# Turning the sink probabilities with VectorE and GpSimd blocks in place of TensorE transposes

## The chip, the cores and the metric

One core of one Trainium2 chip runs the whole program. The metric is the device time of one execution in microseconds (us). The kernel before takes 730.89 us (median of 3 runs, 730.44 to 731.45).

## What is computed

Attention with a few sink positions and a sliding window, then a feed-forward block over the result. q, k and v are 4 batches x 8 heads x 768 positions x 64; `n_sink` is 4 and `window` is 128. Cut to what matters:

```python
scores = (1 / np.sqrt(D)) * q @ k.transpose(0, 1, 3, 2)
keep = (pos[None, :] < n_sink) | ((rel >= 0) & (rel < window))
a = softmax(np.where(keep, scores, -1e9))
x = (a @ v).transpose(0, 2, 1, 3).reshape(B * S, H * D)      # 3072 x 512
h = x @ w_in                                                 # 512 -> 2048
out = (h * sigmoid(h)) @ w_out                               # 2048 -> 512
```

## The kernel before

The 3072 tokens are cut into 8 chunks of 384 (batch, half of the sequence). A chunk goes through two stages: attention for its four pairs of heads (32 periods p = 0 to 31, four to a chunk), then the feed-forward block over its 16 slices of d_ff (`mlp1`, `act`, `mlp2`). The attention of one chunk is computed while the feed-forward block of the chunk before it runs, so that the two share the engines.

The first two chunks (periods 0 to 7, `f_...` functions) do attention in a simpler way; the change does not touch it. From period 8 on (24 periods) each operand is split in two parts, a rounded one (type F32R, "hi") and the rest ("lo"), and products are made of both. For one period, with two heads j = 0 and 1:

- `q_prep`, `k_prep` (lines 387 to 428): VectorE turns 32x32 blocks of q and k into PSUM, ScalarE writes the hi part, VectorE the lo part, and two copies (lines 402, 403) by GpSimd or, from period 15 on, by VectorE.
- `v_prep` (430): the split of v, and of the v rows of the sink slots (`vsn`, NS = 8 slots for each head) into `vk`; vsn holds its rows twice, for the hi and the lo part of P.
- `scores` (451): 2 products for each 128-row tile, reduced by VectorE into `pm`, whose row of 264 holds 128 columns of the window's block before, 8 sink slots and 128 own columns.
- `softmax` (493): ScalarE's exp, VectorE adds the first 128 columns to the own ones (line 502), GpSimd multiplies the own columns by 1/sum (505), and line 508 writes the sink slots of P, scaled, into a small tile `sx`, 8 slots for each head and tile.
- `ptrans` (513): three TensorE transposes of the own columns, ScalarE (528) and VectorE (530) split them, and GpSimd's affine selects (535, 539) part them in two triangles, four for each head.
- `strans` (544): the sink slots of both heads, 16 columns a tile, are transposed by TensorE (line 550, one for each of 3 tiles, or 2 in the first half of a sequence, t0 = 1) into a PSUM bank `sk`; ScalarE (557) writes the hi part to partitions 0 to 15 of `pst`, VectorE (558) the lo part to partitions 32 to 47.
- `av` (562): products of v with the triangles (577, 586) and one more, line 593, of `vk` with `pst`, all into one PSUM bank, which lines 601 to 605 evict. Each head waits for `pst`.

Of the 24 periods, 16 lie in a second half (3 tiles) and 8 in a first half (2 tiles).

The order of the work is set by a planner at the end of the function (lines 930 to 997): each stage is given a due time in units, where one unit is one slice of the feed-forward block (`mlp1` and `mlp2`); all stages are sorted by their time and emitted in that order. The times of attention stand in `OPT["a"]`, relative to T of the period, four units to a period: `st` for strans, `av0` and `av1` for the two heads of av, `q`, `k`, `v`, `s`, `sm` for the preparations, scores and softmax. A scheduler below takes that order as priority, so that an instruction that is ready may pass one that is not; on each engine the instructions then run in the order that it left. GpSimd, VectorE, ScalarE and TensorE each have one queue, and all loads and stores here go through SP's.

Of the kernel before, what the change touches and what calls it, by code (L numbers as in the profile page):

```python
# [8 lines left out]
F32 = mybir.dt.float32  # L9
F32R = mybir.dt.float32r  # L10
I32 = mybir.dt.int32
AF = mybir.ActivationFunctionType
ALU = mybir.AluOpType
# [7 lines left out]
NS = 8  # L21
# [5 lines left out]
OPT = dict(  # L27
    S=7.901, s0=0.903, f_l=2.468, f_p=-1.643, f_v=3.079, f_sm=0.693, f_pt=0.795, f_av=0.251,
    tk=15.973, s1=1.65, F1=1.024, D0=2.076, w=[0.458, 8.623, 11.237, 18.573], wd=[0.85, 0.58,
    1.293, 0.67], wc=19.252, wcd=2.681, warm=7, wg=4, ord=1, edge=8, dua=15, adp=0, glp=0,  # L30
    ptv=7, fill=[0, 4, 0, 0, 1, 0, 0, 2], na=[2, 16], lod=[6, 32], nv=[0, 0], hid=[0, 0],
    ktd=[0, 0], a=dict(load=-3.44, q=-0.196,
    k=-0.079, v=1.975, s=1.356, sd=0.613, sm=1.795, smd=0.457, pt0=2.725, st=3.866, pt1=3.355,
    av0=4.289, av1=4.426), m0=dict(act=0.108, m2=1.206), m=dict(act=1.023, m2=1.546), fin=0.772,
)


# [132 lines left out]
def attn_moe_kernel(  # L170
# [11 lines left out]
    nc = tc.nc  # L182
    B, H, S, D = q.shape
# [5 lines left out]
    P = 128  # L189
    HP = H // 2  # L190
    CT = 384
    NTB = CT // P
# [10 lines left out]
    ident = const.tile([P, P], F32, name="ident")  # L203
# [26 lines left out]
    with ExitStack() as fast:  # L230
        wpool = fast.enter_context(tc.tile_pool(name="wpool", bufs=1))
        p1 = fast.enter_context(tc.tile_pool(name="p1", bufs=1))
# [3 lines left out]
        ps_a = fast.enter_context(tc.tile_pool(name="ps_a", bufs=3, space=PSUM))  # L236


        m0 = p1.tile([P, P], F32, name="m0")
        m1 = p1.tile([P, WIN], F32, name="m1")  # L240
        m2 = p1.tile([P, WIN], F32, name="m2")
        rel = p2.tile([P, P], F32, tag="xh0", name="rel")
        col = p2.tile([P, P], F32, tag="xh1", name="col")
        sk = p2.tile([P, P], F32, tag="xh2", name="sk")
# [39 lines left out]
        ksA = p1.tile([P, HP, B, NS], F32R, name="ksA")  # L284
        ksB = p1.tile([P, HP, B, NS], F32R, name="ksB")

        vsn = p1.tile([48, H, D], F32, tag="vsn2", name="vsn")


        zero = {}  # L290
# [40 lines left out]
        st = [dict() for _ in range(NPER)]  # L331


        turns = [(b, half) for b in range(B) for half in range(NHALF)]
# [3 lines left out]
        def geo(p):  # L338
            c, hp = divmod(p, HP)
            b, half = turns[c]  # L340
            return c, b, half, hp
# [36 lines left out]

        def load_vs(b):
            for j in range(2):  # L380
                for r in (0, 32):
                    nc.sync.dma_start(
                        vsn[r + 8 * j : r + 8 * j + 8, j::2, :],
                        v[b, j::2, 0:NS, :].rearrange("h j d -> j h d"),
                    )
# [19 lines left out]
        def k_prep(p):  # L405
# [11 lines left out]
            for j, src in ((0, ksA), (1, ksB)):  # L417
# [4 lines left out]
                )  # L422
            A = ksv[:, 0, j0:, :P]
            Bk = ksv[:, 1, j0:, :P]
# [5 lines left out]
        def v_prep(p):  # L430
            c, b, half, hp = geo(p)
            s = st[p]
            j0 = 0 if half else 1
            vs = p1.tile([P, NTB + 1, 2, 2, D], F32R, tag="vs", name=f"vs{p}")
            s["vs"] = vs
            vn = s["vn"]
            for j in range(2):
                nc.scalar.copy(vs[:, j0:, j, 0, :], vn[:, j0:, j, :])  # L438
            for j in range(2):
                nc.gpsimd.tensor_tensor(  # L440
                    vs[:, j0:, j, 1, :], vn[:, j0:, j, :], vs[:, j0:, j, 0, :], ALU.subtract
                )
            if "vk" not in zero:
                zero["vk"] = p1.tile([P, 2, 2, D], F32R, tag="vk", name="vk")
                nc.gpsimd.memset(zero["vk"].bitcast(F32), 0.0)
            vk = zero["vk"]
            src = vsn[:, 2 * hp : 2 * hp + 2, :]
            nc.scalar.copy(vk[:48, :, 0, :], src)
            nc.gpsimd.tensor_tensor(vk[:48, :, 1, :], src, vk[:48, :, 0, :], ALU.subtract)

        def scores(p, j):
            c, b, half, hp = geo(p)
# [40 lines left out]
        def softmax(p, j):  # L493
            c, b, half, hp = geo(p)
            s = st[p]
            pm = s["pma", j]
            t0 = 0 if half else 1
            r = exps(p, j)

            own = pm[:, t0:, SEG:]  # L500
            eng = nc.gpsimd if p < OPT["adp"] else nc.vector
            eng.tensor_tensor(own, own, pm[:, t0:, :P], ALU.add)
            for t in range(NTB):
                x = pm[:, t, SEG:]
                nc.gpsimd.tensor_scalar(x, x, r[:, t : t + 1], 1.0, ALU.mult, ALU.mult)  # L505
            if j == 0:
                s["sx"] = p1.tile([P, NTB, 2, NS], F32, tag="sx", name=f"sx{p}")
            nc.gpsimd.tensor_tensor(
                s["sx"][:, t0:, j], pm[:, t0:, P : P + NS],
                r[:, t0:].unsqueeze(2).to_broadcast([P, NTB - t0, NS]), ALU.mult,  # L510
            )

# [29 lines left out]
                )  # L542

        def strans(p):
            c, b, half, hp = geo(p)
            s = st[p]
            t0 = 0 if half else 1
            pt = ps_a.tile([P, 512], F32, tag="at", name=f"sk{p}")
            for t in range(t0, NTB):
                nc.tensor.transpose(  # L550
                    pt[0 : 2 * NS, t * P : (t + 1) * P],
                    s["sx"][:, t].rearrange("p h j -> p (h j)"),
                    ident,
                )
            ps = zero["pst"]
            src = pt[0 : 2 * NS, t0 * P : CT]
            nc.scalar.copy(ps[0 : 2 * NS, t0 * P :], src)
            nc.vector.tensor_tensor(
                ps[32 : 32 + 2 * NS, t0 * P :], src, ps[0 : 2 * NS, t0 * P :], ALU.subtract
            )  # L560

        def av(p, j):
            c, b, half, hp = geo(p)
            s = st[p]
            if j == 0:
                s["x32"] = p1.tile([P, 4 * P], F32, tag="x32", name=f"x32_{p}")
            o = ps_a.tile([P, 512], F32, tag="at", name=f"o{p}_{j}")
            pq = s["pq", j].rearrange("p t o x q -> p (t o) x q")

            todo = [(1, 1, 3, 0), (2, 3, 5, P)] + [(0, 0, 1, 0)] * half  # L570
            merge = p >= OPT["edge"]
            if not merge:
                todo.append((3, 5, 6, 2 * P))
            first = True
            for kb, b0, b1, q0 in todo:
                for x in range(2):
                    nc.tensor.matmul(  # L577
                        o[:, q0 : q0 + (b1 - b0) * P].rearrange("p (b q) -> p b q", q=P),
                        s["vs"][:, kb, j].rearrange("p a d -> p (a d)"),
                        pq[:, b0:b1, x],  # L580
                        start=first, stop=False, skip_group_check=True,
                    )
                    first = False
            if merge:

                nc.tensor.matmul(  # L586
                    o[:, 2 * P : 4 * P],
                    s["vs"][:, NTB, j].rearrange("p a d -> p (a d)"),
                    pq[:, 5].rearrange("p x q -> p (x q)"),
                    start=False, stop=False, skip_group_check=True,  # L590
                )
            t0 = 0 if half else 1
            nc.tensor.matmul(  # L593
                o[:, t0 * P : CT],
                zero["vk"][:, j].rearrange("p a d -> p (a d)"),
                zero["pst"][:, t0 * P :],
                start=False, stop=True, skip_group_check=True,
            )
            x32 = s["x32"][64 * j : 64 * j + 64]
            n = 4 * P if merge else CT  # L600
            nc.scalar.copy(x32[:, :n], o[64:128, :n])
            nc.vector.tensor_tensor(x32[:, :n], o[0:64, :n], x32[:, :n], ALU.add)
            if merge:
                nc.vector.tensor_tensor(
                    x32[:, 2 * P : CT], x32[:, 2 * P : CT], x32[:, CT:], ALU.add
                )
            if j == 1:
                s["xh"] = p2.tile([P, CT], F32R, tag=f"xh{hp}", name=f"xh{p}")
                s["xl"] = p2.tile([P, CT], F32R, tag=f"xl{hp}", name=f"xl{p}")
                x32 = s["x32"][:, :CT]  # L610
                nc.scalar.copy(s["xh"], x32)
                nc.vector.tensor_tensor(s["xl"], x32, s["xh"], ALU.subtract)
# [16 lines left out]
        for n in range(2):  # L629
            zero["pT", n] = p2.tile([P, 2, 2 * NTB, P], F32, tag="pq", name=f"pTz{n}")  # L630
            nc.gpsimd.memset(zero["pT", n][:, :, 2], 0.0)
        FP = 2 * HP

        def f_load(p):
            c, b, half, hp = geo(p)
# [295 lines left out]
        for p in range(NPER):  # L931
            T = O["S"] + 4.0 * (p - HP)
            c, b, half, hp = geo(p)
            if p < FP:
                for j in range(2):
# [20 lines left out]
                       lambda p=p, j=j: in_turn(lambda: f_av(p, j)))  # L956
                continue
            A = O["a"]

            tl = T - 4.0 + max(A["k"] + 0.05, 4.0 + A["load"])  # L960
            tv = T - 4.0 + max(A["v"] + 0.05, 4.0 + A["load"])
            at(tl, lambda p=p: load(p))
            at(tv, lambda p=p: load_v(p))
            if hp == 0 and (c == 2 or b != turns[c - 1][0]):
                at(max(tv, O["tk"]) + 0.02, lambda b=b: load_vs(b))
            at(T + A["q"], lambda p=p: q_prep(p))
            at(T + A["k"], lambda p=p: k_prep(p))
# [66 lines left out]
```

## Time and profile before

| | us |
|---|---|
| median of 3 runs | 730.89 |
| lowest, highest | 730.44, 731.45 |
| the profiled execution | 731.18 |
| its span, first to last instruction | 729.4 |

The span covers 12276 instructions; the mean granted TensorE clock over it is 0.995 of full speed. In the rows, PE is TensorE's matmul, PEld its weight load, DVE is VectorE, ACT ScalarE, POOL GpSimd. Line numbers (L550) are those of the kernel before. `x16` behind a row is a count of instructions. The chain of waits follows the work that ended last back from the last instruction, at each step to what released it; its pieces carry the time that each adds to the chain. A busy TensorE is not TensorE at its peak, because the ends of matmuls are modelled; the chain's pieces and the starts are the better guide.

### The profile page before, as it was taken

What the parts mean: (1) busy time and instruction counts of PE and PEld (TensorE: products, weight loads), DVE (VectorE), ACT (ScalarE), POOL (GpSimd) and SP (SyncE); (2) the same over time, 40 slices, a digit from 0 to 9 for tenths busy, and PEclk for the clock granted to TensorE, in tenths of its full rate; (3) what the DMA queues carried; (4) which work ended last, traced back from release to release, by engine and by line L of the source; (5) the groups of instructions that cost most, each with busy time, mean ns of one, the idle gap of its engine ahead of it and who ended that gap; (6) DMA issues with size and microseconds to landing.
All of it is one profiled execution on the core that took longest, in us unless ns stands there. A gap on an engine that the chain in (4) does not pass through costs nothing.

```text
span 729.4 us, 12276 instructions
## 1 busy us (share of the span) xinstructions
PE 714.4 (98%) x3906; PEld 629.8 (86%) x3906; DVE 489.7 (67%) x1323; ACT 498.3 (68%) x1165; POOL 249.1 (34%) x547
## 2 busy tenths in 40 slices
PE   7998999999999999999999999999999999999997
PEld 5676788798999999899999998999898989998986
DVE  5899767977767687667867777677866776731111
ACT  4889788776776777777676767777677777732112
POOL 3310000155444564534334545333443453320000
PEclk8999999999999999999999999999999999999999
DMA  7556446535322542124322352115421321001001
GB/s 177 178 156 183 139 119 164 158 85 147 96 40 41 137 116 61 27 60 133 86 40 40 99 144 62 29 32 164 120 40 26 98 68 32 1 0 44 1 2 45
DMA packets 141333, 61.87 MB, mean 85 GB/s; under 512 B 130000, under 2 KB 130000, under 8 KB 141264
## 3 DMA queue, kind: packets, MB, share of 16 engines
q1 hardware_dynamic: 140976, 61.04, 32.8%
q8 instruction: 32, 0.52, 0.3%
q14 instruction: 37, 0.30, 0.1%
q10 hardware_dynamic: 288, 0.00, 0.0%
HBM read 54.72 MB, written 6.29 MB: 84 GB/s over the span
## 4 chain that ended last, share of the span: by engine, by line
PE 88%; DMA 4%; DVE 4%; ACT 2%; SPq 1%; issue 1%; POOL 0%; DVEq 0%; ACTq 0%
PE h L854 35%; PE out L882 12%; PE out L881 12%; PE out L880 12%; PE o L577 4%; PE s L464 2%; PE s L468 2%; PE o L790 2%; PE pt L519 2%; DMA wraw<-in_moe_w_in_dram 2%; DMA wraw<-in_moe_w_out_dram 2%; PE o L593 1%; PE o L586 1%; PE sk L550 1%; DVE wcv L43 1%; PE s L722 1%
## 5 line engine op out<-in xcount | busy, mean ns | idle before, releaser
L854 PE MATMUL h<-xh,winh 128*128 128x384 f32 x512 | 178.3, 348 | 0.0
L854 PE MATMUL h<-xl,winh 128*128 128x384 f32 x512 | 173.8, 339 | 0.0
L854 PE MATMUL h<-xh,winl 128*128 128x384 f32 x512 | 173.7, 339 | 0.0
L880 PE MATMUL out<-wouth,gh 128*128 128x512 f32 x384 | 153.5, 401 | 1.7 <-ACT gh L865 1.6
L881 PE MATMUL out<-woutl,gh 128*128 128x512 f32 x384 | 152.4, 397 | 0.3 <-DVE woutl L830 0.2
L882 PE MATMUL out<-wouth,gl 128*128 128x512 f32 x384 | 149.9, 396 | 0.1
L865 ACT ACTIVATE gh<-h 128x384 fp32r<-128x384 f32 x128 | 63.1, 493 | 113.7 <-PE h L854 109.8
L868 DVE TENSOR_TENSOR gl<-sg,gh 128x384 fp32r<-128x384 f32 x128 | 73.5, 574 | 88.6 <-ACT sg L866 86.1
L854 PEld LDWEIGHTS h<-xh,winh 128*128 128x128 f32 x512 | 96.5, 188 | 3.5 <-issue 0.9
L854 PEld LDWEIGHTS h<-xl,winh 128*128 128x128 f32 x512 | 96.4, 188 | 2.1
L854 PEld LDWEIGHTS h<-xh,winl 128*128 128x128 f32 x512 | 96.0, 188 | 0.5 <-issue 0.3
L882 PEld LDWEIGHTS out<-wouth,gl 128*128 128x128 f32 x384 | 71.8, 188 | 17.4 <-DVE gl L868 0.8
L880 PEld LDWEIGHTS out<-wouth,gh 128*128 128x128 f32 x384 | 72.2, 188 | 14.6 <-ACT gh L865 2.4
L881 PEld LDWEIGHTS out<-woutl,gh 128*128 128x128 f32 x384 | 72.2, 188 | 12.8 <-DVE woutl L830 1.1
L472 DVE CUSTOM_DVE_ANT_0 pm<-s,m 128x264 f32<-128x264 f32 (+1 forms) x144 | 53.7, 409 | 35.2 <-PE s L468 35.2
L485 ACT ACTIVATE pm<-pm,mx 128x264 f32<-128x264 f32 (+1 forms) x144 | 70.9, 494 | 2.7
L505 POOL TENSOR_SCALAR pm<-pm,r 128x128 f32<-128x128 f32 x144 | 59.0, 427 | 32.6 <-DVE r L490 29.9
L440 POOL TENSOR_TENSOR vs<-vn,vs 128x256 fp32r<-128x256 f32 (+1 forms) x48 | 34.3, 716 | 94.4 <-ACT vs L438 82.5
L866 ACT ACTIVATE sg<-h 128x384 f32<-128x384 f32 x128 | 62.4, 487 | 0.6
L535 POOL TENSOR_SCALAR_AFFINE_SELECT pq<-pq 128x384 fp32r<-128x384 f32 (+1 forms) x96 | 48.2, 502 | 21.0 <-ACT pq L528 20.5
L539 POOL TENSOR_SCALAR_AFFINE_SELECT pq<-pq 128x384 fp32r<-128x384 f32 (+1 forms) x96 | 50.5, 526 | 12.0 <-DVE pq L530 5.6
L530 DVE TENSOR_TENSOR pq<-pt,pq 128x384 fp32r<-128x384 f32 x48 | 26.7, 556 | 30.9 <-ACT pq L528 29.1
(162 smaller groups left out, 1265.8 us busy)
## 6 DMA issues: line engine op xcount, KB each, us to landing
wraw<-in_moe_w_in_dram SPq DMA_DIRECT2D x16, 512.0 KB
wraw<-in_moe_w_out_dram SPq DMA_DIRECT2D x16, 512.0 KB
wchk<-in_moe_w_in_dram SPq DMA_DIRECT2D x16, 512.0 KB
wchk<-in_moe_w_out_dram SPq DMA_DIRECT2D x16, 512.0 KB
qn<-in_q_dram SPq DMA_DIRECT2D x96, 48.0 KB
kn<-in_k_dram SPq DMA_DIRECT2D x64, 64.0 KB
vn<-in_v_dram SPq DMA_DIRECT2D x32, 128.0 KB
out_dram<-ost SPq DMA_DIRECT2D x7, 512.0 KB
```

The source lines that it names most:

```text
L472: nc.vector.tensor_tensor_reduce(out=pm[:, t, off:], in0=sp[:, :w], in1=(m0, m1, m2)[min(blk, 2)], scale=-0.125, scalar=3.0e38, op0=ALU.ad ...
L485: nc.scalar.activation(x, x, AF.Exp, bias=mx[:, p, j * NTB + t : j * NTB + t + 1], scale=-1.0, accum_out=r[:, t : t + 1],)
L505: nc.gpsimd.tensor_scalar(x, x, r[:, t : t + 1], 1.0, ALU.mult, ALU.mult)
L535: nc.gpsimd.affine_select(out=before, in_=own, pattern=[[0, n], [-1, P]], compare_op=ALU.is_gt, fill=0.0, base=0, channel_multiplier=1,)
L539: nc.gpsimd.affine_select(out=own, in_=own, pattern=[[0, n], [1, P]], compare_op=ALU.is_ge, fill=0.0, base=0, channel_multiplier=-1,)
L854: nc.tensor.matmul(hps[:, :CT], w[g][:, cc, fs], s[x], start=n == 0, stop=n == 3 * NCC - 1)
L865: nc.scalar.activation(gh, hps[:, :CT], AF.Silu)
L866: nc.scalar.activation(sg, hps[:, :CT], AF.Silu)
L868: eng.tensor_tensor(gl, sg, gh, ALU.subtract)
L880: nc.tensor.matmul(o, gh[:, ts_], wout_h[g][:, f], start=fc == 0, stop=False)
L881: nc.tensor.matmul(o, gh[:, ts_], wout_l[g][:, f], start=False, stop=False)
L882: nc.tensor.matmul(o, gl[:, ts_], wout_h[g][:, f], start=False, stop=fc == NFC - 1)
```

## The change

The tile `sx` is gone. The sink slots are written by line 508's instruction into columns that are free after line 502 (the first 128 of `pm` of head 0, tile 1), 32 columns for each tile: 16 for hi, 16 for lo. `strans` then splits them ahead of the turn: ScalarE writes the hi part, GpSimd subtracts to get the lo part, VectorE turns 128 x 96 (or 128 x 64) in 32x32 blocks into columns of `pm` of head 1, and GpSimd copies the four groups of 32 partitions side by side to partitions 0 to 31 of `pst`. In `pst` the columns now lie by group, tile and column; line 593's product reads them in runs of 32, in the order of its output. `vsn` shrinks from 48 to 32 partitions. TensorE has no instruction left in `strans`. The times of several stages move, and three assertions on the order are added.

```diff
-    ktd=[0, 0], a=dict(load=-3.44, q=-0.196,
-    k=-0.079, v=1.975, s=1.356, sd=0.613, sm=1.795, smd=0.457, pt0=2.725, st=3.866, pt1=3.355,
-    av0=4.289, av1=4.426), m0=dict(act=0.108, m2=1.206), m=dict(act=1.023, m2=1.546), fin=0.772,
+    ktd=[0, 0], a=dict(load=-3.44, q=0.257, k=-0.012, v=1.813, s=1.461, sd=0.613, sm=1.795,
+    smd=0.605, pt0=2.725, st=3.866, pt1=3.355, av0=4.289, av1=4.669), m0=dict(act=0.108,
+    m2=1.206), m=dict(act=1.068, m2=1.546), fin=0.927, FP=8,
...
-        vsn = p1.tile([48, H, D], F32, tag="vsn2", name="vsn")
+        vsn = p1.tile([32, H, D], F32, tag="vsn2", name="vsn")
...
-                for r in (0, 32):
+                for r in (0, 16):
...
-            nc.scalar.copy(vk[:48, :, 0, :], src)
-            nc.gpsimd.tensor_tensor(vk[:48, :, 1, :], src, vk[:48, :, 0, :], ALU.subtract)
+            nc.scalar.copy(vk[:32, :, 0, :], src)
+            nc.gpsimd.tensor_tensor(vk[:32, :, 1, :], src, vk[:32, :, 0, :], ALU.subtract)
...
             if j == 0:
-                s["sx"] = p1.tile([P, NTB, 2, NS], F32, tag="sx", name=f"sx{p}")
+                s["sx"] = pm[:, 1, : 32 * NTB].rearrange("p (t x h j) -> p t x h j", x=2, h=2, j=NS)
             nc.gpsimd.tensor_tensor(
-                s["sx"][:, t0:, j], pm[:, t0:, P : P + NS],
+                s["sx"][:, t0:, 1, j], pm[:, t0:, P : P + NS],
                 r[:, t0:].unsqueeze(2).to_broadcast([P, NTB - t0, NS]), ALU.mult,
             )
...
         def strans(p):
-            c, b, half, hp = geo(p)
-            s = st[p]
-            t0 = 0 if half else 1
-            pt = ps_a.tile([P, 512], F32, tag="at", name=f"sk{p}")
-            for t in range(t0, NTB):
-                nc.tensor.transpose(
-                    pt[0 : 2 * NS, t * P : (t + 1) * P],
-                    s["sx"][:, t].rearrange("p h j -> p (h j)"),
-                    ident,
-                )
-            ps = zero["pst"]
-            src = pt[0 : 2 * NS, t0 * P : CT]
-            nc.scalar.copy(ps[0 : 2 * NS, t0 * P :], src)
-            nc.vector.tensor_tensor(
-                ps[32 : 32 + 2 * NS, t0 * P :], src, ps[0 : 2 * NS, t0 * P :], ALU.subtract
-            )
+            s = st[p]
+            t0 = 0 if geo(p)[2] else 1
+            hi, x = (s["sx"][:, t0:, n].rearrange("p t h j -> p t (h j)") for n in range(2))
+            nc.scalar.copy(hi.bitcast(F32R), x)
+            nc.gpsimd.tensor_tensor(x, x, hi, ALU.subtract)
+            su = s["pma", 1][:, 0, : 32 * (NTB - t0)]
+            nc.vector.transpose(su, s["sx"][:, t0:].rearrange("p t x h j -> p (t x h j)"))
+            ps = zero["pst"][0:32].rearrange("k (i c) -> k i c", i=4)[:, :, 32 * t0 :]
+            for i in range(4):
+                nc.gpsimd.tensor_copy(ps[:, i], su[32 * i : 32 * i + 32])
...
             nc.tensor.matmul(
-                o[:, t0 * P : CT],
+                o[:, t0 * P : CT].rearrange("p (t i c) -> p t i c", i=4, c=32),
                 zero["vk"][:, j].rearrange("p a d -> p (a d)"),
-                zero["pst"][:, t0 * P :],
+                zero["pst"].rearrange("p (i t c) -> p t i c", i=4, c=32)[:, t0:],
                 start=False, stop=True, skip_group_check=True,
             )
...
-        FP = 2 * HP
+        FP = OPT["FP"]
...
-            if hp == 0 and (c == 2 or b != turns[c - 1][0]):
+            if p == FP or hp == 0 and b != turns[c - 1][0]:
                 at(max(tv, O["tk"]) + 0.02, lambda b=b: load_vs(b))
```

## Rows read from the trace of the kernel before

**Rows 1.** Page: busy time of each engine, share of the span, instructions.

```profile
PE 714.4 (98%) x3906; PEld 629.8 (86%) x3906; DVE 489.7 (67%) x1323; ACT 498.3 (68%) x1165; POOL 249.1 (34%) x547
```

**Rows 2.** Busy time by stretch: length, PE, PEld, DVE, ACT, POOL, PEclk, DMA share, GB/s.

```profile
445.00:545.00 100.00, 100.00 (x567) 90.74 (x566) 72.30 (x197) 72.19 (x173) 44.99 (x105) 1.00 0.29 70
645.00:729.40 84.40, 79.07 (x400) 70.64 (x398) 14.16 (x28) 19.61 (x43) 0.00 (x0) 0.99 0.06 20
```

**Rows 3.** Chain of waits from 145 to 650 us, share by line.

```profile
by line: PE h L854 40.1%; PE out L881 13.3%; PE out L882 13.3%; PE out L880 13.3%; PE o L577 5.6%; PE s L464 3.4%; PE s L468 3.4%; PE pt L519 3.2%; PE o L593 1.5%; PE o L586 1.5%; PE sk L550 1.4%
```

**Rows 4.** Chain, period 21 (3 tiles): start, length in us, line, count.

```profile
433.32 0.33 PE sk L550 x3
433.65 2.11 PE h L854 x12
...
436.57 0.17 PE o L593
...
439.84 2.12 PE h L854 x12
441.95 0.12 PE s L464
```

**Rows 5.** Chain, period 19 (2 tiles), the same columns.

```profile
391.44 0.22 PE sk L550 x2
...
393.76 0.47 PE o L577 x4
...
394.35 0.12 PE o L593
```

**Rows 6.** ACT and DVE by line and shape: busy us, mean ns, then idle before.

```profile
L557 ACT CAST pst<-sk 16x384 fp32r<-16x384 f32 x16 | 7.5, 467 | 7.8 <-PE sk L550 7.8
L557 ACT CAST pst<-sk 16x256 fp32r<-16x256 f32 x8 | 2.9, 363 | 2.4 <-PE sk L550 2.4
...
L390 DVE STREAM_TRANSPOSE qt<-qn 128x384 f32<-128x384 f32 x24 | 14.0, 582 | 0.0
L410 DVE STREAM_TRANSPOSE kt<-kn 128x512 f32<-128x512 f32 x16 | 11.6, 722 | 0.4
L558 DVE TENSOR_TENSOR pst<-sk,pst 16x384 fp32r<-16x384 f32 x16 | 8.8, 547 | 1.8 <-ACT pst L557 1.3
```

**Rows 7.** POOL, single lines: count, duration ns min/median/max, first and last start, shapes.

```profile
L508 POOL TENSOR_TENSOR sx<-pm,r x48: 215/450/604, 154.1 to 638.6; 128x24 f32<-128x24 f32 x32, 128x16 f32<-128x16 f32 x16
L449 POOL TENSOR_TENSOR vk<-vsn,vk x24: 451/456/614, 130.9 to 629.1; 48x128 fp32r<-48x128 f32 x24
L402 POOL CAST qd<-qd x7: 499/500/945, 143.1 to 265.9; 64x384 fp32r<-64x384 f32 x7
L419 POOL CAST ks<-ksA x24: 197/204/335, 101.2 to 613.3; 128x24 fp32r<-128x24 f32 x16, 128x16 fp32r<-128x16 f32 x8
```

**Rows 8.** Timeline of ACT and of POOL, period 21: start us, length us.

```profile
428.80 0.48 ACT L528 CAST pq<-pt 128x384 fp32r<-128x384 f32 x1
...
428.85 0.54 POOL L508 TENSOR_TENSOR sx<-pm,r 128x24 f32<-128x24 f32 x1
429.36 0.97 POOL L535 TENSOR_SCALAR_AFFINE_SELECT pq<-pq 128x384 fp32r<-128x384 f32 x1
...
434.18 0.52 POOL L539 TENSOR_SCALAR_AFFINE_SELECT pq<-pq 128x384 fp32r<-128x384 f32 x1
```

**Rows 9.** Timeline of POOL and PE, period 8, the first of the 24.

```profile
157.03 0.22 POOL L508 TENSOR_TENSOR sx<-pm,r 128x24 f32<-128x24 f32 x1
...
162.02 0.75 POOL L539 TENSOR_SCALAR_AFFINE_SELECT pq<-pq 128x384 fp32r<-128x384 f32 x1
162.63 0.34 PE L593 MATMUL o<-pst,vk 128*128 128x384 f32 x1
```

**Rows 10.** Timeline of DVE, period 21: q's first and k's last preparation.

```profile
430.34 0.58 DVE L390 STREAM_TRANSPOSE qt<-qn 128x384 f32<-128x384 f32 x1
...
438.07 0.69 DVE L428 TENSOR_TENSOR ks<-kt,ks 64x512 fp32r<-64x512 f32 x1
```

More of the change, by code (lines that the diff above doesn't have):

```diff
@@ L958, in attn_moe_kernel @@
             A = O["a"]
+            assert max(A["q"], A["k"]) < A["s"] and A["s"] + A["sd"] < A["sm"] + A["smd"]
+            assert A["s"] < A["sm"] < A["pt0"] and A["sm"] + A["smd"] < min(A["pt1"], A["st"])
+            assert max(A["v"], A["pt0"], A["st"]) < A["av0"] < A["av1"] and A["pt1"] < A["av1"]
             tl = T - 4.0 + max(A["k"] + 0.05, 4.0 + A["load"])
```

## The prediction

> **What bounds the kernel now.** I read the page's busy shares first: TensorE is at 98%, VectorE and ScalarE at two thirds, GpSimd at 34% [rows 1]. Since a share is a mean over stages, the stretches come next. Where attention and the feed-forward block run together, TensorE is busy for 100.00 of 100 us at a granted clock of 1.00, that is 2.4 GHz, while GpSimd has 45 of 100 us of work; four other stretches of 100 us between 145 and 645 us look the same. After 645 us there is no attention left, and GpSimd does nothing [rows 2]. A busy TensorE is not yet a bound, so the chain of waits decides: from 145 to 650 us its pieces are all TensorE's, and the shares by line add up to the whole [rows 3]. So in these 505 us each piece of TensorE's work is worth its length, and work on the other engines is worth nothing until it makes TensorE wait. All 24 calls of strans lie in this stretch.
>
> **What goes.** The chain shows what the transposes cost: 0.33 us for three of them [rows 4], 0.22 us for two [rows 5]. The twelve products behind them take 2.11 us, and 2.12 us where no transpose stands ahead [rows 4], so nothing more is hidden in what follows. Sixteen periods by 0.33 and eight by 0.22 make 5.28 + 1.76 = 7.04 us. As a check, the share of line 550, 1.4% of 505 us, is 7.1 us [rows 3]. I take all of it as gained. The Trainium skill (TensorE: Matmul & The Clock Gate, Back-to-back issue gap) has about 81 ns for a product of 128 columns in a sustained stream; 64 of them would be an estimated 5.2 us, and the sum below would come out 1.8 us higher. The row has 110 ns for each, and it decides.
>
> ScalarE's copy of 467 ns and VectorE's subtraction of 547 ns out of PSUM go too [rows 6], and a PSUM bank of the rotating three is free for longer. TensorE waits for none of these banks in this stretch [rows 3], so I put that at nothing; at best it shortens waits outside it, and I keep half a microsecond for that below the forecast.
>
> **What comes, for a period of three tiles.** ScalarE's hi copy has 48 columns: from 467 ns at 384 and 363 ns at 256 columns a line gives 0.19 us [rows 6]; the ends are 0.19 and 0.36. GpSimd's subtraction of 48 columns lies between 215 ns at 24 and 456 ns at 128 columns: 0.27 us; the ends are 0.22 and 0.60, the longest of line 508 [rows 7]. VectorE's turn of 96 columns, from 582 ns at 384 and 722 ns at 512 [rows 6], is 0.27 us; the upper end is 0.58. GpSimd's four copies of 96 columns with a shift of partitions, between 204 ns at 24 and 500 ns at 384 columns, where line 402 shifts partitions as well [rows 7], are 0.26 us each, 1.05 in all; the ends are 0.82 and 2.00. From one engine to the next I take at most 0.08 us, from the end of line 528 on ScalarE (429.28) to GpSimd's select at 429.36 [rows 8]; four such steps are 0.32. In sum 0.19 + 0.27 + 0.27 + 1.05 + 0.32 = 2.1 us, one behind the other, and 4.0 us with every upper end.
>
> **What hides it.** The sink slots are ready when line 508 of the second head ends, at 429.39 us [rows 8]; the first product that reads pst is at 436.57 us [rows 4], and without the transposes it would be wanted 0.33 us earlier, at 436.24. That is 6.85 us for a chain of 2.1 to 4.0 us. But it shares GpSimd's queue with the eight affine selects, the last of which ends at 434.70 us [rows 8]. GpSimd's new work, 0.27 + 1.05 = 1.32 us, put behind them, would end at 436.0 us: in time, with 0.2 us to spare, if the turn is done by then. If selects go behind copies, the second head's products wait for them; its due time has moved from 4.426 to 4.669, behind the mlp2 at 4.622, so they have about 2 us more. On VectorE a turn of 0.27 takes the place of 0.55 us, on ScalarE 0.19 that of 0.47. GpSimd's total grows by 24 times 1.3, some 32 us, in a queue that is idle more than half of the time [rows 2].
>
> The first period is tighter: from 157.25 us to the product at 162.63 us, GpSimd is at selects until 162.77 us [rows 9]. There 1.32 us more may come straight on to TensorE; the copies of q_prep leave this stretch, so I take half, 0.6 us, once (ends 0 and 1.3).
>
> **The sink product's new reading order.** Line 593 reads 12 runs of 32 columns (8 in a first half) instead of one run; its output stays in order. The trace has no such read. The nearest row: four products of 256 columns in two runs take 0.47 us, 0.118 each; one of 256 in one run takes 0.12 [rows 5]. So a second run costs nothing that shows, and I take 0; a gain is excluded, as nothing gets shorter. The other end: 128 columns more cost 0.05 us (0.17 against 0.12) [rows 4, 5], so 256 cost 0.10, and a fixed 0.018 of the 0.118 remains. If all of that were due to the two runs, 0.009 each, twelve runs would add 0.09 us and eight 0.05 to each product: 32 by 0.09 and 16 by 0.05 are 3.7 us, all on the chain.
>
> **The rest, with one answer.** q_prep moves later by 0.453 units, behind strans and k_prep; its VectorE part begins at 430.34 us and k's last step ends at 438.76 us [rows 10], while the next scores come at 441.95 us [rows 4], so 3.2 us cover it; a rival below prices their loss. softmax, v_prep, act, and the copies at a chunk's end move by 0.05 to 0.25 units on engines that have over a quarter of their time free [rows 2]. The four loads of the sink rows of v keep number and size; load_v is emitted earlier by 0.16 units, and SP's queue has a DMA share of 0.29 to carry [rows 2]. All of these: 0.
>
> **The sum.** 731.18 us (the profiled execution, 729.4 us of it the span) - 7.04 + 0.6 = 724.74; that execution stands 0.29 us above the median, so 724.5 us.
>
> **The rivals.**
> - *GpSimd is late.* If the subtraction itself stands behind the last select, the chain starts at 434.70: 0.27 + 0.27 + 1.05 and 0.24 for the steps end at 436.53 us, 0.3 late against 436.24, and TensorE stops in front of line 593 with all that is queued behind it. Line 508 takes from 215 to 604 ns [rows 7]; one such stretch of 0.39 in five new instructions makes it 0.68 us. Over the 16 periods of three tiles that is 10.9 us: 735.4 us, slower. The point from which it decides is a mean stop of 0.29 us a period, 7.04 / 24. For it: how little is spare behind the selects; against it: nothing makes the subtraction wait for a select, and an instruction that is ready may pass. The Trainium skill (SBUF — State Buffer, Who interferes with whom) holds that a VectorE instruction with two inputs in SBUF and a GpSimd one that reads SBUF shut each other out; by that rule several of the five would be stretched, an estimated 2 us at 0.39 each. Chance 0.14.
> - *The scores are late.* Some five VectorE instructions of q_prep, about 0.55 us each by rows of their kind [rows 6], land between k_prep and the scores: 438.76 + 2.7 - 0.28 = 441.2 us. With two evictions of the av bank ahead of them, about 0.55 each, that is 442.3 against 441.6 wanted: 0.7 us late, in 16 periods 11 us, 735.7 us. Against it: VectorE took line 390 three microseconds ahead of strans [rows 4, 10], so ready work is pulled forward. Chance 0.07.
> - *The runs of 32 cost their upper end:* 724.5 + 3.7 = 728.2 us, still faster. Chance 0.08.
> - *Small stops take half of the gain* without either queue being late throughout: about 728 us. Chance 0.05.
> - That the transposes stay is excluded by the diff: no call on TensorE is left in strans.
>
> **How the numbers follow.** The forecast, 723 to 726.5 us, has 0.66. About 0.2%, 1.5 us, is what a measurement of this kernel can tell from no change. Forecast, runs and small stops are faster: 0.79. Of the two late cases some 0.05 land within 0.2%, the remaining 0.16 above. The range reaches down to 722.5 (no stop in the first period, the half microsecond of the banks, the scatter of about 1 us between the runs) and up to 731.5, which takes in the runs of 32 and the small stops and leaves out most of the two late cases.
>
> **What would show it.** Right: the chain has no line 550, TensorE is still busy for all of each 100 us, the whole is shorter by 0.33 and 0.22 us a period, VectorE's turn is near 0.27 us, and GpSimd's copies of 96 columns near 0.26. Wrong: idle time of TensorE ahead of line 593 that ends with GpSimd's copy, or ahead of the scores that ends with VectorE's preparation; pieces of line 593 longer than 0.17 us; GpSimd's copies above 0.5 us, where the chain no longer fits behind the selects.

## The result and the profile after

The changed kernel takes 724.12 us (median of 4 runs, 723.44 to 725.18) against 731.17 us for the kernel before on the same chips: ratio 0.9905, 95% interval 0.9888 to 0.9923, so faster by 7 us. The profiled execution took 723.66 us, its span 721.8 us.

In the changed kernel the numbers of lines shift: 551 is strans' hi copy on ScalarE, 552 its subtraction and 558 its four copies on GpSimd, 554 VectorE's turn, 591 the sink product (593 before), 575 the products with the triangles (577), 536 and 540 the affine selects (535, 539), 852 mlp1 (854), 878 to 880 mlp2 (880 to 882).

The page's busy times, which answer to [rows 1]:

```profile
PE 705.0 (98%) x3842; PEld 624.1 (86%) x3842; DVE 481.3 (67%) x1323; ACT 489.4 (68%) x1165; POOL 281.5 (39%) x667
```

Busy time by stretch, with the columns of [rows 2]:

```profile
145.00:245.00 100.00, 99.45 (x559) 90.91 (x558) 71.33 (x191) 73.87 (x174) 59.12 (x137) 1.00 0.35 85
...
445.00:545.00 100.00, 100.00 (x567) 91.67 (x566) 71.52 (x198) 71.52 (x170) 50.40 (x129) 1.00 0.28 66
```

TensorE makes 64 products fewer and is as full as before; GpSimd is busy for 32 us more, as forecast. In the first stretch TensorE is idle for 0.55 us, which it was not before.

The chain of waits from period 22 on (start, length, line), which answers to [rows 4]:

```profile
451.03 2.10 PE h L852 x12
453.13 0.64 PE o L575 x6
...
453.94 0.18 PE o L591
454.12 0.23 PE out L878
```

No piece of line 550 is left. A period can be measured from its first sink product to that of the next one. From period 22 to 23 the timelines have, in the kernel before and then in the changed one:

```profile
457.70 0.34 PE L593 MATMUL o<-pst,vk 128*128 128x384 f32 x1
...
478.99 0.34 PE L593 MATMUL o<-pst,vk 128*128 128x384 f32 x1
```

```profile
453.78 0.34 PE L591 MATMUL o<-pst,vk 128*128 128x384 f32 x1
...
474.69 0.34 PE L591 MATMUL o<-pst,vk 128*128 128x384 f32 x1
```

That is 21.29 us before and 20.91 us now: 0.38 us less, not 0.33.

The new instructions by line and shape (busy us, mean ns, then idle before):

```profile
L558 POOL CAST pst<-pm 32x96 fp32r<-32x96 f32 x64 | 17.9, 279 | 2.3
...
L552 POOL TENSOR_TENSOR pm<-pm 128x48 f32<-128x48 f32 x16 | 4.7, 293 | 4.4 <-ACT pm L551 4.1
...
L554 DVE STREAM_TRANSPOSE pm<-pm 128x96 f32<-128x96 f32 x16 | 4.5, 278 | 10.0 <-POOL pm L552 10.0
...
L551 ACT CAST pm<-pm 128x48 fp32r<-128x48 f32 x16 | 3.9, 241 | 8.0 <-POOL pm L509 7.3
```

The terms were 0.26 for a copy, 0.27 for the subtraction, 0.27 for the turn and 0.19 us for the hi copy. In 19 of the 23 later periods the chain from the hi copy to the end of the last copy takes 2.1 to 2.8 us; in periods 12, 20 and 28 it takes 3.3 us, and in period 9 it takes 5.4 us, with selects among its steps. It is done 1.5 us ahead of line 591 in period 9 and 2.5 to 5 us ahead of it in the others.

In period 8 it is not. Of the chain of waits there, the last copy and then the sink product:

```profile
162.45 0.57 POOL pst L558
...
163.06 0.44 PE o L591
```

And of the list of waits of the changed kernel from 145 to 645 us (total, times, longest):

```profile
PE o L591 <- POOL pst L558: 0.5, 1, 0.5
PEld o L575 <- POOL pq L540: 0.4, 1, 0.4
```

These two are all of any size that TensorE waits for in the 500 us: the first period's stop, taken as 0.6 us and measured at 0.5 us (0.7 for its weight load), and a weight load's wait of 0.4 us in period 21, where line 575 of the first head waits for a select. That period is 0.4 us longer than others of its kind (21.33 against 20.91 us).

### The profile page after: what moved, and what is told of

Same layout as the page of the kernel before. It is cut to its first block, busy times and chain, and to the rows that moved or that the text cites. A ratio compares the mean times of both kernels' runs of the same rounds, so it can differ in the third digit from the quotient of the medians.

```text
span 721.8 us, 12275 instructions
## 1 busy us (share of the span) xinstructions
PE 705.0 (98%) x3842; PEld 624.1 (86%) x3842; DVE 481.3 (67%) x1323; ACT 489.4 (68%) x1165; POOL 281.5 (39%) x667
## 4 chain that ended last, share of the span: by engine, by line
PE 81%; DMA 5%; DVE 5%; ACT 3%; POOL 2%; issue 2%; SPq 1%; DVEq 0%; POOLq 0%; ACTq 0%
PE h L852 32%; PE out L880 11%; PE out L879 11%; PE out L878 11%; PE o L575 4%; DMA wraw<-in_moe_w_in_dram 3%; PE o L788 2%; PE s L468 2%; PE s L464 2%; PE pt L520 2%; DMA wraw<-in_moe_w_out_dram 2%; PE o L591 1%; DVE wcv L43 1%; DVE wcv L42 1%; PE o L584 1%
## 5 line engine op out<-in xcount | busy, mean ns | idle before, releaser
L866 DVE TENSOR_TENSOR gl<-sg,gh 128x384 fp32r<-128x384 f32 x128 | 75.4, 589 | 87.2 <-ACT sg L864 84.9
L505 POOL TENSOR_SCALAR pm<-pm,r 128x128 f32<-128x128 f32 x144 | 61.5, 442 | 42.5 <-DVE r L490 39.2
L600 DVE TENSOR_TENSOR x<-o,x 64x512 f32<-64x512 f32 x48 | 32.8, 683 | 35.5 <-ACT x L599 34.4
L419 POOL CAST ks<-ksA 128x24 fp32r<-128x24 f32 (+1 forms) x24 | 4.8, 201 | 131.7 <-PE s L468 73.0
L438 ACT CAST vs<-vn 128x256 fp32r<-128x256 f32 (+1 forms) x48 | 18.6, 388 | 50.1 <-PE o L584 49.6
```

The lines of the kernel that those rows point to most:

```text
L866: eng.tensor_tensor(gl, sg, gh, ALU.subtract)
```

## The experiments

Theory A is the prediction's: the gain is the transposes that TensorE no longer makes, and all else lies beside other work. Theory B: it is the new due times by themselves. Ratios are to the kernel before, run on the same chip.

**The changed kernel with the old due times.**

```diff
-    q=0.257, k=-0.012, v=1.813, s=1.461, ... smd=0.605, ... av1=4.669 ... m=dict(act=1.068, ...), fin=0.927
+    q=-0.196, k=-0.079, v=1.975, s=1.356, ... smd=0.457, ... av1=4.426 ... m=dict(act=1.023, ...), fin=0.772
```

> The changed kernel with every due time of the kernel before (q, k, v, s, smd, av1, act, fin put back). Theory A, the gain is the transposes that TensorE no longer makes: 724 to 726 us, ratio 0.990 to 0.993, with at most some waits more in front of the second head's products, since av1 again follows av0 at once and the selects have GpSimd's copies ahead of them. Theory B, the gain comes from the new times: 730 us or more, ratio above 0.998. In between, 727 to 729 us: the copies displace the selects and the new times are what hides it.

Measured: 730.64 us (11 runs, 728.57 to 732.81), ratio 0.9995 (0.9984 to 1.0006). With the old times the change wins nothing, as theory B had it and not theory A. The list of waits says why (total, times, longest):

```profile
PEld o L575 <- POOL pq L540: 4.3, 4, 2.1
PE o L575 <- POOL pq L540: 3.3, 4, 1.9
PEld o L591 <- POOL pst L558: 2.1, 1, 2.1
PE o L591 <- POOL pst L558: 1.9, 1, 1.9
```

TensorE's products stop for GpSimd: 1.9 us in period 8 and, ahead of the second head's products, 0.7, 0.4, 0.4 and 1.9 us in periods 9, 10, 12 and 13, together 5.2 us; from period 14 on nowhere. The timeline of period 13, GpSimd's work and the products of line 575 (start, length):

```profile
269.94 0.52 POOL L536 TENSOR_SCALAR_AFFINE_SELECT pq<-pq 128x384 fp32r<-128x384 f32 x1
...
270.52 0.50 POOL L402 CAST qd<-qd 64x384 fp32r<-64x384 f32 x1
...
271.09 0.52 POOL L540 TENSOR_SCALAR_AFFINE_SELECT pq<-pq 128x384 fp32r<-128x384 f32 x1
...
271.56 0.52 POOL L536 TENSOR_SCALAR_AFFINE_SELECT pq<-pq 128x384 fp32r<-128x384 f32 x1
...
271.86 0.28 PE L575 MATMUL o<-pq,vs 128*128 128x256 f32 x1
...
272.15 0.88 POOL L403 CAST qd<-qd 64x384 fp32r<-64x384 f32 x1
...
273.10 0.86 POOL L540 TENSOR_SCALAR_AFFINE_SELECT pq<-pq 128x384 fp32r<-128x384 f32 x1
...
274.01 1.12 PE L575 MATMUL o<-pq,vs 128*128 128x256 f32 x5 [1.87 <-POOL pq L540]
```

Among the selects stand lines 402 and 403, q_prep's copies, which GpSimd makes up to period 14 alone. And the stop costs more than its length, as the stretches of this run show (PEclk is the column after POOL's):

```profile
272.00:274.00 2.00, 0.14 (x2) 0.00 (x0) 1.97 (x5) 0.59 (x2) 1.82 (x3) 1.00 0.78 104
274.00:276.00 2.00, 1.99 (x9) 1.90 (x10) 1.33 (x3) 0.49 (x2) 0.03 (x1) 0.57 0.00 0
276.00:278.00 2.00, 2.00 (x7) 1.57 (x6) 1.32 (x2) 1.19 (x4) 1.70 (x3) 0.58 0.00 0
278.00:280.00 2.00, 2.00 (x12) 1.87 (x11) 0.56 (x1) 0.43 (x1) 0.20 (x1) 1.00 0.54 122
```

For 4 us after the idle stretch the mean granted clock is 0.57, that is for most of the time the lower level, 1.2 GHz: some 1.7 us more. The stop in period 8, which ended at 163.39 us, has the same behind it:

```profile
166.00:168.00 2.00, 2.00 (x6) 1.60 (x5) 1.36 (x4) 0.83 (x3) 1.25 (x2) 0.50 0.00 0
```

The clock is at 0.76 in the 2 us ahead of this stretch and at 0.88 in the 2 us behind it, again some 1.7 us lost. This execution has 4.6 us more of stops than the changed kernel's (5.2 against 0.6) and 3.4 us of slow clock, together 8.0 us, and its span is 7.5 us longer (729.3 against 721.8). So stops and clock account for the gain that is lost, to half a microsecond. This made theory D: q's place, ahead of the selects in GpSimd's queue, is what undoes the gain.

**The kernel before with the new due times** (the same lines the other way round).

> The kernel before with every due time of the changed one; strans stays on TensorE. Theory A: 730 to 733 us, ratio 0.998 to 1.003, TensorE without idle time from 145 to 645 us, so that no order of the same work can be faster there. Theory B: 724 to 726 us.

Measured: 734.5 us, ratio 1.005 (1.0037 to 1.0064): slower, also than the 730 to 733 us of theory A. Theory B is out: in the kernel before the new times are a loss by themselves. In the list of waits TensorE now waits for VectorE's subtraction in strans and for selects:

```profile
PE o L577 <- DVE pst L558: 2.2, 3, 1.0
PEld o L577 <- POOL pq L539: 1.6, 2, 1.3
```

**Idle transposes put back into the changed kernel.**

```diff
+            pt = ps_a.tile([P, 512], F32, tag="at", name=f"sk{p}")
+            for t in range(t0, NTB):
+                nc.tensor.transpose(
+                    pt[0 : 2 * NS, t * P : (t + 1) * P], s["pm", 1][t][:, SEG : SEG + 2 * NS], ident
+                )
```

> The changed kernel with 64 transposes of 16 columns put back on TensorE in strans, into a bank of the rotating three that nothing reads (the columns turned are P's own ones, ready long before). Theory A: 724.1 + 16 x 0.33 + 8 x 0.22 = 731.1 us, 730 to 732, ratio 0.999 to 1.002, all of the gain gone although nothing waits for them. Theory B, or transposes that lie beside other work: 724 to 726 us.

Measured: 733.26 us, ratio 1.0037 (1.0023 to 1.0051). All of the gain goes, and 2 us more than theory A's 731.1: in this profile TensorE waits 0.9 us ahead of line 464 for the eviction of av, a wait that the changed kernel does not have. From period 22 to 23 it has:

```profile
459.25 0.34 PE L596 MATMUL o<-pst,vk 128*128 128x384 f32 x1
...
480.51 0.34 PE L596 MATMUL o<-pst,vk 128*128 128x384 f32 x1
```

That is 21.25 us (the starts are rounded), 0.35 us more than in the changed kernel, and a period of two tiles (18 to 19) is 0.25 us longer. So 64 products that nobody reads cost their time on TensorE, which is theory A; whether the rest is due to the PSUM bank they take was not told apart.

**The kernel before without strans.**

```diff
         def strans(p):
-            c, b, half, hp = geo(p)
...
+            return
```

> The kernel before with strans left out altogether (no transposes, no copy, no subtraction; pst stays zero, so the sink slots' part of the product is missing). Theory A: 731.2 - 7.0 = 724.1 us, 723.3 to 725, ratio 0.989 to 0.992: the same as the changed kernel within a microsecond, since ScalarE's and VectorE's part lay beside other work. If the split on ScalarE and VectorE, or the PSUM bank, held TensorE up as well: below 723 us.

This kernel leaves out the sink slots' part of the result. Measured: 724.54 us, ratio 0.9913 (0.9898 to 0.9928): 6.2 to 6.4 us, and with it the changed kernel's time. With the old times and no transposes, GpSimd's queue is the old one and the gain is there. One wait of 1.0 us ahead of mlp2 for VectorE is in its profile. From period 22 to 23 it has:

```profile
453.10 0.34 PE L578 MATMUL o<-pst,vk 128*128 128x384 f32 x1
...
474.04 0.34 PE L578 MATMUL o<-pst,vk 128*128 128x384 f32 x1
```

That is 20.95 us (rounded), 0.35 us less than in the kernel before; a period of two tiles (18 to 19) is 0.21 us shorter.

**One old time at a time.** The changed kernel with the old times, and:

```diff
-    q=-0.196
+    q=0.257
```

> The changed kernel with the old times, but q at 0.257, so that q_prep stands behind strans again. Theory D: with the old times the two copies of q_prep on GpSimd (lines 402, 403, in periods 8 to 14 alone) stand ahead of affine selects in GpSimd's queue; together with strans' five new instructions they make the selects late, TensorE stops, and its clock falls. Then this one time gives most of the gain back: 724 to 727 us, ratio 0.990 to 0.995. Theory E, it is the later av1 that hides the selects: 729 to 731 us, as with all the old times.

Measured: 723.65 us, ratio 0.9893 (0.9878 to 0.9908): all of the gain, from this one number. In period 13 GpSimd's timeline has the copies behind the last select:

```profile
267.18 0.72 POOL L540 TENSOR_SCALAR_AFFINE_SELECT pq<-pq 128x384 fp32r<-128x384 f32 x1
267.97 0.50 POOL L402 CAST qd<-qd 64x384 fp32r<-64x384 f32 x1
268.53 0.51 POOL L403 CAST qd<-qd 64x384 fp32r<-64x384 f32 x1
```

```diff
-    av1=4.426
+    av1=4.669
```

> The changed kernel with the old times, but av1 at 4.669, so that the second head's products come behind one more mlp2. Theory E: 724 to 726 us. Theory D: the waits ahead of line 575's second head (2.0 + 0.9 + 0.5 + 0.5 us with the old times) mostly go, the wait of 2.1 us ahead of line 591 in period 8 and the slower clock behind it stay: 727 to 729 us.

Measured: 733.11 us, ratio 1.0027 (1.0017 to 1.0037). Both theories' times missed: the waits ahead of the second head do go, the one of 1.9 us in period 8 stays, but a new one comes (from the list of waits):

```profile
PE out L880 <- DVE gl L866: 4.9, 7, 1.2
PE o L591 <- POOL pst L558: 1.9, 1, 1.9
```

Theory E, that the later av1 hides the selects, is out. With av1 late and q early, mlp2 waits for its gl part from VectorE, up to 1.2 us at a time.

```diff
-    dua=15
+    dua=8
```

> The changed kernel with all the old times, but q_prep's two copies on VectorE from period 8 on, not from period 15 on (dua = 8). Theory D: 724 to 726 us, ratio 0.990 to 0.994, with no idle time of TensorE over 0.5 us between 145 and 645 us, because GpSimd's queue in periods 8 to 14 is then like that of the later periods, which have no such waits under the old times. Theory E: 729 to 731 us, since av1 still follows av0 at once.

Measured: 724.76 us, ratio 0.9911 (0.9896 to 0.9926). With every old time, the two copies moved from GpSimd to VectorE in seven periods bring the gain. This and the run with q alone show theory D from two sides.

**GpSimd's copies made twice**, in the changed kernel.

```diff
-            for i in range(4):
+            for i in range(4 * 2):
+                i = i % 4
                 nc.gpsimd.tensor_copy(ps[:, i], su[32 * i : 32 * i + 32])
```

> The changed kernel with each of strans' four GpSimd copies made twice, 1.1 us more of GpSimd's work a period (same data, same result). Theory A, the copies lie beside TensorE's work from period 9 on, with 1.5 to 5 us to spare ahead of line 591: 724 to 727 us, ratio to the kernel before 0.990 to 0.995, some waits in periods 8 to 14 alone. Theory C, GpSimd's queue is all but the bound: 0.5 to 1 us a period, 736 us or more, waits in all periods.

Measured: 728.19 us, ratio 0.9958 (0.9943 to 0.9973), between the two theories. TensorE's products stop for 1.8 us in period 8, 0.2 in 9, 1.1 in 13 and 0.2 in 21, 3.3 us together (4.6 us by the waits of the weight loads) and in no period after 21. That is 2.7 us more than in the changed kernel (3.5 by the weight loads) for a time that is 4.1 us longer; the rest was not traced. So GpSimd has a microsecond to spare in the periods after 21 and lacks it in periods 8, 9 and 13.

**The sink product's reading order**, in the changed kernel. Here the sink slots' part lands in the wrong columns of the sum; the number of products and columns is the same.

```diff
-                o[:, t0 * P : CT].rearrange("p (t i c) -> p t i c", i=4, c=32),
+                o[:, t0 * P : CT],
                 zero["vk"][:, j].rearrange("p a d -> p (a d)"),
-                zero["pst"].rearrange("p (i t c) -> p t i c", i=4, c=32)[:, t0:],
+                zero["pst"][:, t0 * P :],
```

> The changed kernel with line 591's product reading pst as one run of columns again, so that the sink slots' part lands in the wrong columns of the sum (the same number of columns and products). Theory A, runs of 32 cost nothing: the same as the changed kernel, 723.5 to 725 us, pieces of the product of 0.17 and 0.12 us as before. Rival, each run costs up to 9 ns: up to 3.7 us faster, 720.5 us.

Measured: 723.94 us, ratio 0.9886 (0.9869 to 0.9902). The changed kernel's time; its interval leaves out the rival's gain of 3.7 us on 724.1 (a ratio of 0.985). The pieces of the chain agree, in this run and then in the changed kernel (first half of a sequence, 256 columns):

```profile
391.79 0.12 PE o L591
```

```profile
391.16 0.12 PE o L591
```

**q late in the kernel before.**

```diff
-    q=-0.196
+    q=0.257
```

> The kernel before with q alone at 0.257. Theory D, q's place matters only because GpSimd's queue is fuller in the changed kernel: here the selects had room, so nothing is won, 730 to 732.5 us, ratio 0.998 to 1.002; a loss of 1 to 4 us if it is q's place that made the kernel before with all new times slower (VectorE's subtraction in strans late). Theory B, a later q is worth several us by itself: 724 to 727 us.

Measured: 742.68 us, ratio 1.0149 (1.0132 to 1.0166), a loss of 11 us, far over the 1 to 4 us that theory D had for it. The list of waits:

```profile
PEld o L577 <- issue: 8.9, 19, 1.8
PE o L577 <- DVE ks L428: 3.5, 6, 0.7
```

The timeline of one period (VectorE's line 428 is k_prep's last step, the reader of a PSUM bank that line 577's sum does not read):

```profile
443.78 0.39 PE L880 MATMUL out<-wouth,gh 128*128 128x512 f32 x1
...
444.01 0.69 DVE L428 TENSOR_TENSOR ks<-kt,ks 64x512 fp32r<-64x512 f32 x1
...
444.85 0.89 PE L577 MATMUL o<-pq,vs 128*128 128x256 f32 x6 [0.68 <-DVE ks L428]
```

The second head's sum waits for k_prep, from which it takes no data; what they share is the rotation of three PSUM banks, in which q's, k's and strans' banks now stand together. In the changed kernel strans takes none, and q at the same place costs nothing. In this period line 428 ends at 444.70 us, 1.1 us behind the start of the first sink product; in the run with q alone it ends 1.4 us ahead of it (431.06 and 432.49). So k_prep runs later here. That the bank holds it up is an inference: most of the waiting is put down to "issue", VectorE's queue, with strans' subtraction in it, is a rival that was not told apart, and the kernel before with all new times has q at the same place and the same banks and loses 3.7 us, not 11. What a fourth bank would give was not tried, and where all 11 us go stays open.

**A version with copies on ScalarE**, from the run with q alone (two copies; then all four).

```diff
             for i in range(4):
-                nc.gpsimd.tensor_copy(ps[:, i], su[32 * i : 32 * i + 32])
+                if i % 2:
+                    nc.scalar.copy(ps[:, i], su[32 * i : 32 * i + 32])
+                else:
+                    nc.gpsimd.tensor_copy(ps[:, i], su[32 * i : 32 * i + 32])
```

> The changed kernel with the old times but q at 0.257, and two of strans' four copies made by ScalarE. Theory D: GpSimd's queue loses 0.55 us a period, the two waits that are left (0.6 us ahead of line 591 in period 8, 0.4 us ahead of line 575 in period 13) shrink or go: 722.5 to 723.7 us, at best a microsecond below the same kernel with all four on GpSimd. Rival: ScalarE, whose queue is fuller than GpSimd's, puts its share behind other work and delays the product: 724 to 727 us.

Measured: 723.01 us, ratio 0.9875 (0.9858 to 0.9891). The two waits of the run with q alone (0.6 us in period 8, 0.3 in 13) are gone, and the chain from 145 to 645 us is TensorE's alone:

```profile
by line: PE h L855 40.8%; PE out L881 13.4%; PE out L882 13.4%; PE out L883 13.4%; PE o L578 5.6%; PE s L468 3.5%; PE s L464 3.4%; PE pt L520 3.2%; PE o L594 1.5%; PE o L587 1.5%; PE o L791 0.3%
```

> The same with all four copies made by ScalarE, some 0.25 us each, 1.0 us a period. Theory D: as with two, 722.5 to 724 us, no wait for line 558's copies or for selects over 0.3 us. Rival, ScalarE becomes the late queue: its copies stand between exp and the evictions of av, TensorE waits ahead of line 591 or for a bank: 725 us or more.

Measured: 723.15 us, ratio 0.9883 (0.9866 to 0.9900). ScalarE is not the late queue either. Both lie about half a microsecond below the run with q alone (723.65) and one below the changed kernel, as the waits would have it; the intervals overlap, so which is fastest is not settled.

## Why the prediction was right, and where it was not

**What goes:** the sum had 7.04 us; the kernel before without strans gave 6.2 to 6.4 us with a new wait of 1.0 us in it, the changed kernel 7.0. By the periods, taking out three transposes shortens one by 0.35 us and putting three back lengthens it by 0.35; for two it is 0.21 and 0.25. Sixteen and eight periods of these make 7.2 to 7.5 us, so the term held within half a microsecond. Each transpose was worth 103 to 123 ns, near the row's 110, and not the 81 ns of the Trainium skill (TensorE: Matmul & The Clock Gate, Back-to-back issue gap). Idle transposes cost all of the gain again, so the mechanism stands.

The changed kernel wins a little more than that. From the first sink product of period 8 to that of period 31 it is 162.63 to 646.70 us before and 163.06 to 639.46 after: 484.07 and 476.40, 7.67 us less in 23 periods, although period 21 has lost 0.4 us. Without that loss a period is shorter by 0.35 us on the mean ((7.67 + 0.4) / 23), where the sum had 0.29 (7.04 / 24). The part that is not the transposes', some 0.04 us in a period of three tiles, lies in mlp1: from period 22 to 23 its twelve products take 2.10 to 2.11 us each time on the chain, and 2.11 to 2.13 before; why was not found. Periods 25 and 26 win 0.2 us each on top, of which the cause stays open too. The stops in period 8 and period 21 took back one microsecond, where the sum had 0.6.

**What comes and what hides it:** 2.1 us for the chain, with an upper end of 4.0 (its terms add up to 3.9); 2.1 to 2.8 measured in 19 of 23 periods, 3.3 in three, and 5.4 in period 9, outside the bounds, without a stop ahead of line 591. The Trainium skill (SBUF — State Buffer, Who interferes with whom) lets a VectorE instruction with two inputs in SBUF and a GpSimd one that reads SBUF shut each other out; by that rule the prediction had an estimated 2 us. In the 19 periods all that runs beside the chain stretches it by 0.7 us at most; what stretches it in the other four was not told apart from selects that run in between. The 0.6 us of period 8 came as forecast, behind the selects. In the later periods the order did not: there the copies stand ahead of four to seven of the eight selects, so what can be late is a select and the products of line 575, first head included, not line 591.

**The reading order:** 0, and the run with one run of columns agrees. (Twelve runs are eleven more than one and eight are seven more, so the rival's price should have been 4.2 us and not 3.7.)

**The step that failed** is "The rest, with one answer ... All of these: 0". The due times are not free moves: without them the changed kernel takes 730.64 us. The step read only what q's move could delay (the scores) and not what its old place would displace: the prediction costed GpSimd's 1.32 us against the spare time of period 21, where q's copies run on VectorE, and took them to leave the stretch in period 8, while they also share GpSimd's queue in periods 9 to 14. The rival "GpSimd is late" was the right mechanism with the wrong trigger. It does not need the subtraction to wait for a select, only five more instructions and two copies in one queue, and its price in period 13, for example, is the stop of 1.9 us and the slow clock after it. The 0.14 given to it was for a kernel whose new times keep it off; with the old times it is what happens. So the time came out right in part by luck: the prediction counted on room in GpSimd's queue that the new times, which it put at nothing, had made.

**What q's place is worth** depends on strans: late, it costs 11 us in the kernel before and wins 7 us in the changed one. The prediction put the PSUM bank that strans no longer takes at nothing. That the bank is the reason for the 11 us is not shown. The late place is one way to the gain and not the only one, since the copies on VectorE bring it with q at its old place.

**The scores** were not late: no wait ahead of line 464 stands in the changed kernel's list.

## What to carry to other kernels

Where one engine is busy for all of a stretch, the pieces of the chain price what is taken off it, here to some hundredths of a microsecond a period. What is put on an idle engine must be costed against the fullest stretch of that engine's queue, with all its instructions by period, not against its mean share or one typical period. Before a moved due time is costed at nothing, ask what its old place would collide with after the change.

## What was not expected of the hardware

Stops of TensorE of about 1.9 us were followed by some microseconds at the lower clock in three places: both in the run with the old times, as shown above, and one of 1.93 us in the run with the late av1 alone, which ended at 165.00 us and had 0.53 and 0.62 in the stretches from 166 to 168 and 168 to 170 us. In the run with the doubled copies a stop of 1.84 us, which ended at 164.67 us, was not, and the clock stayed at 1.00 (stretches of that run):

```profile
163.00:165.00 2.00, 0.33 (x2) 0.34 (x3) 1.92 (x4) 0.12 (x1) 1.72 (x6) 1.00 0.67 109
165.00:167.00 2.00, 2.00 (x10) 1.64 (x9) 0.99 (x3) 0.58 (x1) 0.90 (x2) 1.00 0.52 83
```

The kernel with the old times also has the widest scatter of all, 728.57 to 732.81 us in 11 runs. That such stops sometimes cost double would fit this. The mean granted clock of each run points that way but does not settle it: 1.000 with 728.57 us and 0.990 to 0.992 with 731.00, 731.04 and 732.81, but 0.997 with 728.84 and with 730.87 alike. Only one execution of each kernel has a profile, so it was not shown.

GpSimd's small instructions vary: in the changed kernel the 96 copies of line 558 take from 226 to 663 ns, with a median of 254. What stretches the long ones was not looked into.
